# The shared pass up to unit 28 put under manual order with a second table of steps

## The chip, the cores and the metric

The kernel runs on one core of one Trainium2 chip. The metric is the device time of one execution in microseconds (us). The core has five engines with a queue each that runs in order: TensorE (PE; its weight loads are shown as PEld), VectorE (DVE), ScalarE (ACT), GpSimd (POOL) and SyncE (SP), which issues all DMAs here.

## The reference

Four batches of 576 rows with 8 heads of 64 columns go through an attention layer and two feed-forward layers. All is float32, and every large product is made of three matmul passes over high and low halves.

```python
# attention, per batch and head
s = scale * q @ k.T, only where |i - j| < 4        -> softmax -> @ v        # local
q_d, k_d, v_d = means over 4 rows; softmax(q_d @ k_d.T) @ v_d, each row repeated 4 times
x = local + repeated
# layer 1
xn = (x - mean) / sqrt(var + 1e-6) * g_ln
x = x + relu(xn @ w_ch1) @ w_ch2                   # 512 -> 2048 -> 512
# layer 2
h = relu(x.T @ w_tok1) @ w_tok2; u = x + h.T       # 576 -> 256 -> 576
out = u + relu(u @ w_ch1) @ w_ch2                  # 512 -> 1536 -> 512
```

## The kernel before

**Attention** goes by 16 pairs (batch, two heads), n = 0 to 15. Each pair has the steps q_sums and v_sums (GpSimd adds groups of four rows), s_pe (local scores on TensorE), s_max (VectorE), s_exp (ScalarE), d_pe, d_max, d_exp (the same for the means), t_pe and td_pe (transposes), t_copy and td_copy (ScalarE), avd_pe and avd_norm (values of the means), up_write and up_read (a round trip through the DRAM tensor up_scr that repeats the rows), av_pe and av_norm (local values), av_add (GpSimd adds into x).

**Layers 1 and 2** go by 18 chunks of 256 rows, 9 for each layer. A unit is 128 hidden columns of one chunk: g1 (12 matmuls of 128x256, line 629, into a bank of the ring h), a relu on ScalarE (line 635) and its low half on VectorE (line 636), then g2 (6 matmuls of 128x512, line 650, into acc or k). The sequence starts with the shared pass: chunks 0 and 1 in turn with weight unit m = 0 to 13, so that each weight unit is used twice soon after it is made (units 0 to 27), then units 28 to 31 with m = 14 and 15, then chunk by chunk, 252 units in all.

**Weights** arrive as raw 64-bit numbers, 32 pieces of 512 KB for layer 1 (two to a weight unit; piece 2m serves g1, piece 2m + 1 serves g2). A piece is converted in five steps: c_a, c_b, c_c (VectorE, lines 149, 154, 159), c_hi (ScalarE, line 164), c_lo (VectorE, line 167). Raw pieces share three staging buffers, and c_c is the last to read one.

**Order.** A block under `tc.manual_schedule()` gives each engine its instructions in program order. It runs the table START: pairs 0 to 3, pair 4 up to its transposes, the layer norm and transposes of chunks 0 and 1, and pieces 0 to 3. "fill" in it is a matmul without a reader. All else is put in order by the planner of the framework, by program position and by the times that it plans with; it may place such instructions in holes of the manual block. `put(pos, ...)` hangs a step at a unit, and LATER spreads the steps of the pairs over ranges of units. PSUM has four rings of two banks: acc, h, g, k. In the shared pass after START all steps of pairs take banks from g.

```python
for i, (u0, u1) in enumerate(LATER):
    e = later.index((a_values, NP * (i + 2) - 1)) + 1
    for k, (f, n) in enumerate(later[o:e]):
        put(u0 + k * (u1 - u0) / (e - o), f, n)
    o = e
```

Of the kernel before, what the change touches and what calls it, by code (L numbers as in the profile page):

```python
# [8 lines left out]
F32R = mybir.dt.float32r  # L9
I32 = mybir.dt.int32  # L10
ACTF = mybir.ActivationFunctionType
ALU = mybir.AluOpType
# [79 lines left out]
def block_kernel(ctx: ExitStack, tc: tile.TileContext, qk, vw, vg, g_ln, wa, t1, t2, wb, band, out):  # L92
# [215 lines left out]
    def d_pe(n, tag=None):  # L308
        qkd = sts[n].pop("qkd")
        pss = []  # L310
        for h in range(2):
            ps = psg(tag)
            psv = ps[:HG, :2 * SG].rearrange("q (c k) -> q c k", c=2)
            pss.append(psv)
        for c in range(2):
            for h in range(2):
                d = slice(64 * h, 64 * h + 64)
                nc.tensor.matmul(  # L318
                    out=pss[h][:, c, :], lhsT=qkd[d, 0, c * HG:(c + 1) * HG], rhs=qkd[d, 1, :],
                    start=True, stop=True,  # L320
                )
        ld.pop((n, "qk"))
        pending[n, "d"] = pss
# [157 lines left out]
    def av_norm(n, *gs):  # L481
        z = rz[n % 2].unsqueeze(3)
        if gs[0] == 0:
            pending[n, "tmp"] = buf(n, "pt").rearrange("p (t h d) -> p t h d", t=NTL, h=2)
        tmp = pending[n, "tmp"]
        parts = [x for g in gs for x in pending.pop((n, "v", g))]
        for rows, tls, psv in parts:
            nc.vector.tensor_scalar(
                out=z[rows, tls], in0=psv[rows, :, :, D:D + 1], scalar1=1e-9, scalar2=None, op0=ALU.add
            )  # L490
        tls = slice(parts[0][1].start, parts[-1][1].stop)
        nc.vector.reciprocal(out=z[:, tls], in_=z[:, tls])  # L492
        for rows, tls, psv in parts:
            if n < NP:
                shape = [rows.stop - rows.start, tls.stop - tls.start, 2, D]
                nc.vector.tensor_tensor(
                    out=tmp[rows, tls], in0=psv[rows, :, :, :D], in1=z[rows, tls].to_broadcast(shape), op=ALU.mult
                )
                continue
# [122 lines left out]
    def g1(i):  # L622
        c, m = seq[i]
        w = wunit(c, m)
        hp = ps_h.tile([128, 512], F32, tag="h", name="h")
        n = 0
        for kk in range(KD):
            for a, e in PASSES:
                nc.tensor.matmul(  # L629
                    out=hp[:, :CN], lhsT=w[:, 0, a, kk * 128:(kk + 1) * 128], rhs=xT[c][:, kk, e, :],  # L630
                    start=(n == 0), stop=(n == 3 * KD - 1),
                )
                n += 1
        t = ht_p.tile([128, 2, CN], F32R, tag="ht", name="ht")
        nc.scalar.activation(out=t[:, 0], in_=hp[:, :CN], func=ACTF.Relu)  # L635
        nc.vector.scalar_tensor_tensor(  # L636
            out=t[:, 1], in0=hp[:, :CN], scalar=0.0, in1=f32(t[:, 0]), op0=ALU.max, op1=ALU.subtract
        )
        hT[i] = t

    def g2(i):
        c, m = seq[i]
# [130 lines left out]
        base.append(base[-1] + nunits(c))  # L773

    def put(pos, f, *args):
        u, half = divmod(int(2 * pos), 2)
        u = min(u, NSEQ - 1)
        (bg if half else mid)[u].append(lambda: f(*args))

# [51 lines left out]
    def load(n, tag):  # L831
        att_load(n, tag)
# [9 lines left out]
        nc.sync.dma_start(out=grow, in_=g_ln)  # L842
        nc.sync.dma_start(out=mask[:, 1], in_=band[:, 1])

    def s_first(n):
        if n == NP:
            nc.vector.tensor_copy(maskr[1], mask[:, 1])
        s_pe(n, "h")

    def add_run(n, k):  # L850
        if n == NP - 1:
            av_add(n, slice(0, 1) if k == 0 else slice(1, 2), nc.vector)
            if k == 1:
# [9 lines left out]
    def conv_step(k):  # L863
# [7 lines left out]
        q_sums, v_sums, s_max, s_exp, d_max, d_exp, t_pe, t_copy, td_pe, td_copy, avd_pe, avd_norm, up_write,  # L871
        up_read, av_pe, av_norm, load, fill, consts, ln_center, xt_pe, xt_hi, xt_lo,
    )}
    steps.update(
        s_pe=s_first, d_pe=lambda n: d_pe(n, "k"), av_add=add_run, raw=load_unit, st=w_load,
        **{name: conv_step(k) for k, name in enumerate(("c_a", "c_b", "c_c", "c_hi", "c_lo"))},
    )
    with tc.manual_schedule():
# [31 lines left out]
    put(2 * UA - 1.5, rota.__setitem__, slice(None), ["g", "k"])  # L910


    later = []
    for n in range(START_PAIRS, len(order) + 1):
        a = [(f, n) for f in (a_scores, a_down, a_turn, a_turn_down)] if n < len(order) else []
        v = [(f, n - 1) for f in (a_values_down, a_values)] if n > START_PAIRS else []
        later += a[:1] + v[:1] + a[1:2] + v[1:] + a[2:]
    o = 0
    for i, (u0, u1) in enumerate(LATER):
        e = later.index((a_values, NP * (i + 2) - 1)) + 1  # L920
        for k, (f, n) in enumerate(later[o:e]):
            put(u0 + k * (u1 - u0) / (e - o), f, n)
        o = e
# [124 lines left out]
```

## Time and profile before

| what | us |
|---|---|
| median of 3 runs (947.05 to 951.1) | 950.93 |
| the profiled execution, its own time | 952.27 |
| its span, first to last instruction | 950.5 |
| TensorE busy | 916.2 |
| VectorE busy | 447.9 |
| ScalarE busy | 280.6 |
| GpSimd busy | 147.5 |

The span is what the views divide; the execution's own time is 1.77 us longer. Busy time of TensorE counts a matmul at either clock, so a stretch at a low clock is full and slow.

### The profile page before, as it was taken

The numbers are of one execution on the slowest core, as the hardware profiler recorded it, in microseconds if no ns is written. First come the engines' busy times: TensorE is split into PE (matmuls) and PEld (weight loads), VectorE is DVE, ScalarE is ACT, GpSimd is POOL, SyncE is SP. The second block draws the span as 40 slices with busy tenths as digits, with TensorE's granted clock in tenths as the row PEclk, the third lists the DMA queues.
The fourth block names the chain that finished last, engine by engine and source line by source line (L and its number), as shares of the span: only waits on it lengthen the run. The fifth ranks groups of instructions, "written<-read, shape, count | busy, mean of one in ns | idle before, by whom it ended". The sixth has DMA issues, their size and how long they took to land.

```text
span 950.5 us, 17304 instructions
## 1 busy us (share of the span) xinstructions
PE 916.2 (96%) x6702; PEld 801.0 (84%) x6702; DVE 447.9 (47%) x1044; ACT 280.6 (30%) x809; POOL 147.5 (16%) x176
## 2 busy tenths in 40 slices
PE   7879999899999999999999999999999999999998
PEld 5667878778888888888889988787888888999997
DVE  4785788794225252276312267896322322222211
ACT  5444344344443343323111122332112111111111
POOL 6443214213322221111010000111001000000000
PEclk9888999999999999999999999999999999999999
DMA  8653565534232132234212025663212211110100
GB/s 221 183 188 115 157 194 182 169 104 106 83 105 67 47 104 62 67 106 144 73 28 63 23 83 150 190 187 111 57 44 63 51 36 33 45 35 13 44 23 23
DMA packets 113121, 89.78 MB, mean 94 GB/s; under 512 B 73264, under 2 KB 91952, under 8 KB 113040
## 3 DMA queue, kind: packets, MB, share of 16 engines
q1 hardware_dynamic: 113040, 88.68, 32.7%
q8 instruction: 53, 0.87, 0.4%
q14 instruction: 28, 0.23, 0.1%
HBM read 66.62 MB, written 14.16 MB: 85 GB/s over the span
## 4 chain that ended last, share of the span: by engine, by line
PE 78%; DVE 8%; DMA 8%; SPq 2%; ACT 1%; issue 1%; POOL 1%; DVEq 0%; ACTq 0%
PE h L629 33%; PE acc L650 31%; DMA up_scr<-od 2%; DMA st<-in_wb_dram 2%; PE k L650 2%; PE k L729 2%; SPq L586 2%; DMA xr<-x_scr 2%; DVE cv L159 2%; PE g L760 2%; DVE cv L154 1%; PE g L282 1%; PE g L363 1%; PE g L318 1%; PE g L468 1%
## 5 line engine op out<-in xcount | busy, mean ns | idle before, releaser
L629 PEld LDWEIGHTS h<-xt,w 128*128 128x128 f32 x3024 | 395.5, 190 | 25.0 <-ACT w L164 1.9
L629 PE MATMUL h<-xt,w 128*128 128x256 f32 x3024 | 411.8, 284 | 1.6 <-ACT w L164 1.0
L650 PE MATMUL acc<-w,ht 128*128 128x512 f32 x1416 | 378.7, 399 | 8.1 <-ACT ht L635 3.6
L650 PEld LDWEIGHTS acc<-w,ht 128*128 128x128 f32 x1416 | 252.2, 189 | 61.5 <-ACT ht L635 5.7
L636 DVE SCALAR_TENSOR_TENSOR ht<-h,ht 128x256 fp32r<-128x256 f32 x252 | 105.8, 421 | 354.6 <-ACT ht L635 354.3
L635 ACT ACTIVATE ht<-h 128x256 fp32r<-128x256 f32 x252 | 96.4, 383 | 394.0 <-PE h L629 370.4
L714 POOL TENSOR_TENSOR xs<-xr,xs 128x512 fp32r<-128x512 f32 x20 | 26.6, 1330 | 292.4 <-ACT xs L713 292.4
L164 ACT ACTIVATE w<-cv 128x512 fp32r<-128x512 f32 x56 | 35.5, 635 | 70.7 <-DVE cv L159 70.5
L346 POOL TENSOR_TENSOR vg<-vg 72x256 f32<-72x256 f32 x39 | 32.8, 841 | 144.7 <-DMA vg<-in_vg_dram 143.5
L167 DVE TENSOR_TENSOR w<-cv,w 128x512 fp32r<-128x512 f32 x56 | 42.6, 764 | 6.4 <-ACT w L164 6.2
L159 DVE SCALAR_TENSOR_TENSOR cv<-st,cv 128x512 int32<-128x512 int32 (+4 forms) x63 | 42.8, 684 | 0.6
L154 DVE SCALAR_TENSOR_TENSOR cv<-st,cv 128x512 int32<-128x512 int32 (+4 forms) x63 | 42.4, 677 | 0.7
L515 POOL TENSOR_TENSOR x<-x,pt 128x256 f32<-128x256 f32 (+2 forms) x44 | 28.0, 649 | 80.2 <-DMA x<-up_scr 47.9
L729 PE MATMUL k<-xs,t1w 128*128 128x512 f32 (+1 forms) x120 | 33.5, 410 | 2.2 <-ACT xs L713 1.4
L760 PE MATMUL g<-r,t2w 128*128 128x512 f32 x120 | 34.0, 395 | 0.0
L593 ACT ACTIVATE xt<-xt 128x512 fp32r<-128x512 f32 x30 | 19.0, 632 | 50.0 <-DMA xt<-xc 49.9
L149 DVE TENSOR_SCALAR cv<-st 128x512 int32<-128x512 int32 (+4 forms) x63 | 25.8, 412 | 13.8 <-DMA st<-in_wb_dram 8.9
L594 DVE TENSOR_TENSOR xt<-xt 128x512 fp32r<-128x512 f32 x30 | 20.6, 686 | 23.6 <-ACT xt L593 23.5
L650 PE MATMUL k<-w,ht 128*128 128x512 f32 x96 | 27.6, 409 | 0.1
L729 PEld LDWEIGHTS k<-xs,t1w 128*128 128x128 f32 (+1 forms) x120 | 19.1, 188 | 7.2 <-ACT xs L713 2.1
L502 ACT ACTIVATE pt<-g,rz 128x64 f32<-128x64 f32 (+1 forms) x78 | 17.4, 322 | 23.2 <-DVE rz L492 21.8
L760 PEld LDWEIGHTS g<-r,t2w 128*128 128x128 f32 x120 | 20.9, 189 | 3.0
(160 smaller groups left out, 700.6 us busy)
## 6 DMA issues: line engine op xcount, KB each, us to landing
st<-in_wa_dram SPq DMA_DIRECT2D x28, 512.0 KB
st<-in_wb_dram SPq DMA_DIRECT2D x24, 512.0 KB
xt<-xc SPq DMA_DIRECT2D x480, 16.0 KB
qk<-in_qk_dram SPq DMA_DIRECT2D x13, 579.0 KB
x_scr<-x SPq DMA_DIRECT2D x18, 256.0 KB
x<-x_scr SPq DMA_DIRECT2D x9, 512.0 KB
out_dram<-x SPq DMA_DIRECT2D x18, 256.0 KB
vw<-in_vw_dram SPq DMA_DIRECT2D x13, 319.9 KB
```

The costliest lines, as they stand in the source:

```text
L154: nc.vector.scalar_tensor_tensor(out=f, in0=h, scalar=-0x40000000, in1=f, op0=ALU.bitwise_and, op1=ALU.bitwise_or)
L159: nc.vector.scalar_tensor_tensor(out=f, in0=l, scalar=29, in1=f, op0=ALU.logical_shift_right, op1=ALU.bitwise_or)
L164: nc.scalar.activation(out=hi, in_=f.bitcast(F32), func=ACTF.Copy)
L167: nc.vector.tensor_tensor(out=lo, in0=f.bitcast(F32), in1=f32(hi), op=ALU.subtract)
L346: nc.gpsimd.tensor_tensor(out=vd[:, :, :, :D], in0=vd[:, :, :, :D], in1=vgt[:, :, o:o + 128].rearrange("p c (h d) -> p c h d", h=2), op=AL ...
L515: (eng or nc.gpsimd).tensor_tensor(out=x, in0=x, in1=tmp[rows, tl:tl + k].rearrange("p t h d -> p t (h d)"), op=ALU.add)
L629: nc.tensor.matmul(out=hp[:, :CN], lhsT=w[:, 0, a, kk * 128:(kk + 1) * 128], rhs=xT[c][:, kk, e, :], start=(n == 0), stop=(n == 3 * KD - 1),)
L635: nc.scalar.activation(out=t[:, 0], in_=hp[:, :CN], func=ACTF.Relu)
L636: nc.vector.scalar_tensor_tensor(out=t[:, 1], in0=hp[:, :CN], scalar=0.0, in1=f32(t[:, 0]), op0=ALU.max, op1=ALU.subtract)
L650: nc.tensor.matmul(out=acc[c, j], lhsT=t[:, a, j * 128:(j + 1) * 128], rhs=w[:, 1, e, :], start=(m == 0 and n == 0), stop=(last and n == 2),)
L729: nc.tensor.matmul(out=rps[b, m], lhsT=tokw["t1"][rows, a, n, m * 128:(m + 1) * 128], rhs=t[rows, e, :], start=(n == 0 and i == 0), stop=( ...
L760: nc.tensor.matmul(out=ps, lhsT=tokw["t2"][:, a, m, o:o + 128], rhs=r_t[b][:, m, e, :], start=(i == 0), stop=(i == len(ops) - 1),)
```

## The change

START stays. A second table, PASS, follows it in the same manual block. It holds pair 4 from avd_pe on, the pairs 5, 6 and 7 whole, pieces 4 to 31 (their raw loads from piece 7 on and their conversions), the loads of pair 8, g1, relu and low of units 0 to 28, and g2 of units 0 to 27. So relu and low become steps of their own, and so does av_act, the part of av_norm that runs on ScalarE for pairs from 4 on. d_pe of pairs 5 to 7 takes its banks from g, as s_pe does. The loop over units starts at 28, and whatever was hung at an earlier unit (the layer norm and the first transposes of chunk 2) is hung at 28. ln_rstd of chunks 0 and 1 was hung at units 8 and 10 and now stands right behind the block. The steps of the pairs from 8 on are spread over units 28 to 51 and 52 to 82; a_scores and a_down of pair 8 were in the range 1 to 25.

```diff
-LATER = ((1, 25), (26, 51), (52, 82))
+PASS = """
+    g1 0; g1 1; avd_pe 4; relu 0; c_a 4; relu 1; c_b 4; q_sums 5; low 0; low 1; g2 0; c_c 4; avd_norm 4;
+    c_hi 4; raw 3 1; g1 2; c_a 5; up_write 4; c_lo 4; v_sums 5; g2 1; relu 2; c_b 5; low 2; c_c 5; av_pe 4;
+    c_a 6; c_hi 5; raw 4 0; c_b 6; g1 3; c_lo 5; av_z 4; up_read 4; g2 2; relu 3; c_c 6; av_act 4; low 3;
+    c_a 7; g1 4; raw 4 1; c_b 7; c_c 7; c_hi 6; s_pe 5 g; relu 4; raw 5 0; c_lo 6; c_hi 7; g2 3; low 4;
+    av_add 4; s_max 5; g1 5; c_lo 7; s_exp 5; c_a 8; g2 4; c_b 8; c_c 8; relu 5; d_pe 5 g; c_a 9; c_hi 8;
+    raw 5 1; low 5; g1 6; load 6 qk; c_b 9; d_max 5; g2 5; relu 6; low 6; d_exp 5; c_lo 8; g1 7; c_c 9; c_a
...
+    25; relu 26; low 26; c_hi 30; c_a 31; g1 27; c_lo 30; c_b 31; g2 26; relu 27; c_c 31; low 27; c_hi 31;
+    g1 28; c_lo 31; g2 27; relu 28; low 28
+"""
+PASS_UNITS = 28
+
+LATER = ((28, 51), (52, 82))
...
+    def relu(i):
+        hT[i] = t = ht_p.tile([128, 2, CN], F32R, tag="ht", name="ht")
+        nc.scalar.activation(out=t[:, 0], in_=hps[i][:, :CN], func=ACTF.Relu)
+
+    def low(i):
+        hp, t = hps.pop(i), hT[i]
...
     def put(pos, f, *args):
-        u, half = divmod(int(2 * pos), 2)
+        u, half = divmod(int(2 * max(pos, PASS_UNITS)), 2)
...
+        emit(START)
         load(5, "vg")
         load(5, "vw")
+        rota[:] = ["g"]
+        emit(PASS)
     for c in range(2):
-        put(8 + 2 * c, ln_rstd, c)
-    rota[:] = ["g"]
-    a_values_down(NP)
-    a_values(NP)
-    for u in range(2 * UA):
-        bg[u].append(lambda: w_split(NPC // 2))
+        ln_rstd(c)
+    nl[0] = nsp[0] = len(pieces)
...
-    for n in range(START_PAIRS, len(order) + 1):
+    for n in range(2 * NP, len(order) + 1):
...
-    g1(0)
-    for i in range(NSEQ):
+    for i in range(PASS_UNITS, NSEQ):
         if i + 1 < NSEQ:
-            g1(i + 1)
+            for f in (g1, relu, low):
+                f(i + 1)
```

## Rows read from the trace of the kernel before

**Rows 1.** The page: busy time and share of TensorE.

```profile
PE 916.2 (96%) x6702; PEld 801.0 (84%) x6702; DVE 447.9 (47%) x1044; ACT 280.6 (30%) x809; POOL 147.5 (16%) x176
```

**Rows 2.** Windows by stage: busy time of each engine, granted clock, DMA.

```profile
240.00:400.00 160.00, 160.00 (x1407) 140.92 (x1405) 55.97 (x162) 59.46 (x205) 33.12 (x49) 1.00 0.28 75
```

**Rows 3.** Windows in the shared pass: PE, PEld, DVE, ACT, POOL busy, clock.

```profile
86.70:93.80 7.10, 7.10 (x21) 5.36 (x22) 6.16 (x12) 3.85 (x12) 4.67 (x2) 0.53 0.43 143
93.80:188.50 94.70, 88.00 (x740) 75.00 (x739) 76.88 (x167) 40.92 (x120) 29.20 (x28) 1.00 0.56 176
sum 119.00, PE 110.18 PEld 93.56 DVE 91.23 ACT 50.96 POOL 35.94; mean PE 27.54 PEld 23.39 DVE 22.81 ACT 12.74 POOL 8.99
```

**Rows 4.** Waits of TensorE, 69.5 to 188.5 us: total, times, longest.

```profile
PE g L318 <- issue: 2.1, 1, 2.1
...
PE acc L650 <- ACT w L164: 1.7, 3, 0.9
```

**Rows 5.** Timeline of TensorE: start, us, what, idle before.

```profile
86.68 2.23 PE L318 MATMUL g<-qkd 64*72 64x144 f32 x8 [2.12 <-issue]
...
186.47 0.73 PE L650 MATMUL acc<-w,ht 128*128 128x512 f32 x2 [1.76 <-ACT ht L635]
```

**Rows 6.** Window around the gap before 186.47 us.

```profile
185.00:187.00 2.00, 0.53 (x2) 0.30 (x2) 1.97 (x4) 1.06 (x3) 0.00 (x0) 1.00 0.25 53
```

**Rows 7.** Timeline of ScalarE: s_exp of pair 5.

```profile
85.42 2.20 ACT L300 ACTIVATE sm<-g,nm 128x70 f32<-128x70 f32 x10 [2.42 <-DVE nm L292]
```

**Rows 8.** Timeline of TensorE: one whole unit without gaps.

```profile
136.56 1.60 PE L629 MATMUL h<-xt,w 128*128 128x256 f32 x12
138.00 1.55 PE L650 MATMUL k<-w,ht 128*128 128x512 f32 x6
139.38 0.63 PE L629 MATMUL h<-xt,w 128*128 128x256 f32 x4
```

**Rows 9.** Windows of line 629 alone (g1): TensorE busy and count.

```profile
0.00:69.50 69.50, 6.06 (x36) 4.91 (x36) 0.90 0.72 202
```

**Rows 10.** Timeline of TensorE at the end of START.

```profile
64.75 0.59 PE L837 MATMUL acc<-mask,ident 128*128 128x256 f32 x2
65.00 1.89 PE L629 MATMUL h<-xt,w 128*128 128x256 f32 x13
67.70 0.26 PE L384 MATMUL g<-ident,attw 72*72 72x72 f32 x1 [0.82 <-ACT attw L337]
67.89 1.45 PE L629 MATMUL h<-xt,w 128*128 128x256 f32 x10
...
69.36 0.41 PE L384 MATMUL acc<-ident,attw 72*72 72x72 f32 x4
```

**Rows 11.** Timelines of VectorE and ScalarE there: low 0, d_max 4, d_exp 4.

```profile
63.36 0.41 DVE L636 SCALAR_TENSOR_TENSOR ht<-h,ht 128x256 fp32r<-128x256 f32 x1
...
65.94 0.81 DVE L328 TENSOR_REDUCE dm<-k 72x2 f32<-72x288 f32 x2
...
67.27 1.18 ACT L337 ACTIVATE attw<-k,dm 72x144 f32<-72x144 f32 x4 [1.64 <-DVE dm L329]
```

**Rows 12.** Groups by line, VectorE, 69.5 to 188.5: c_a of staged pieces.

```profile
L149 DVE TENSOR_SCALAR cv<-st 128x512 int32<-128x512 int32 x26 | 11.0, 425 | 3.1 <-DMA st<-in_wa_dram 3.1
```

**Rows 13.** Timeline of VectorE: first two steps of ln_rstd.

```profile
107.69 0.16 DVE L556 TENSOR_SCALAR va<-mv 128x2 f32<-128x2 f32 x1
107.88 0.17 DVE L558 TENSOR_SCALAR y<-va 128x2 int32<-128x2 int32 x1
```

**Rows 14.** Timeline of TensorE: chunk 2's second transposes and first g1.

```profile
208.11 0.66 PE L573 MATMUL g<-ident,xc 128*128 128x128 f32 x4 [0.28 <-ACT sm L300]
...
210.78 0.48 PE L629 MATMUL h<-xt,w 128*128 128x256 f32 x2
```

**Rows 15.** By line over the whole run: duration in ns, min/median/max.

```profile
L262 POOL TENSOR_TENSOR qkd<-qkd,qk x13: 932/947/3857, 5.6 to 349.5; 128x288 f32<-128x288 f32 x13
...
L154 DVE SCALAR_TENSOR_TENSOR cv<-st,cv x63: 218/682/1802, 70.0 to 650.4; 128x512 int32<-128x512 int32 x52, 128x256 int32<-128x256 int32 x5, 128x288 int32<-128x288 int32 x2, 128x224 int32<-128x224 int32 x2
```

More of the change, by code (lines that the diff above doesn't have):

```diff
@@ L66 @@
 """
-LATER = ((1, 25), (26, 51), (52, 82))
+PASS = """
[5 more added lines that the diff above has]
+    raw 5 1; low 5; g1 6; load 6 qk; c_b 9; d_max 5; g2 5; relu 6; low 6; d_exp 5; c_lo 8; g1 7; c_c 9; c_a
+    10; c_hi 9; raw 6 0; t_pe 5 0; c_b 10; t_pe 5 1; relu 7; t_copy 5 0; c_lo 9; g2 6; t_copy 5 1; low 7;
+    c_c 10; q_sums 6; t_pe 5 2; td_pe 5 0; t_copy 5 2; c_a 11; g1 8; raw 6 1; td_copy 5 0; c_b 11; c_hi 10;
+    c_c 11; td_pe 5 1; relu 8; c_lo 10; g2 7; raw 7 0; td_copy 5 1; c_hi 11; low 8; c_a 12; avd_pe 5; c_lo
+    11; c_b 12; g1 9; load 6 vg; avd_norm 5; c_c 12; av_pe 5; up_write 5; relu 9; c_a 13; c_hi 12; low 9;
+    raw 7 1; c_b 13; g2 8; load 6 vw; av_z 5; v_sums 6; c_lo 12; g1 10; av_act 5; c_c 13; g2 9; c_a 14;
+    up_read 5; c_b 14; relu 10; c_c 14; c_hi 13; s_pe 6 g; low 10; raw 8 0; c_hi 14; c_lo 13; g1 11; raw 8
+    1; s_max 6; g2 10; relu 11; c_lo 14; s_exp 6; low 11; av_add 5; g1 12; c_a 15; c_b 15; c_c 15; d_pe 6 g;
+    relu 12; c_a 16; c_hi 15; raw 9 0; g2 11; low 12; load 7 qk; d_max 6; g1 13; c_lo 15; d_exp 6; c_b 16;
+    g2 12; relu 13; c_c 16; low 13; c_hi 16; raw 9 1; t_pe 6 0; c_a 17; c_b 17; t_pe 6 1; t_copy 6 0; g1 14;
+    c_lo 16; t_copy 6 1; c_c 17; q_sums 7; t_pe 6 2; relu 14; td_pe 6 0; c_a 18; raw 10 0; t_copy 6 2; g2
+    13; low 14; td_copy 6 0; c_b 18; c_hi 17; c_c 18; td_pe 6 1; g1 15; td_copy 6 1; c_lo 17; raw 10 1; c_hi
+    18; c_a 19; c_lo 18; avd_pe 6; relu 15; low 15; g2 14; c_b 19; load 7 vg; avd_norm 6; g1 16; c_c 19;
+    up_write 6; c_a 20; c_hi 19; c_b 20; av_pe 6; raw 11 0; relu 16; c_lo 19; v_sums 7; low 16; g2 15; load
+    7 vw; c_c 20; av_z 6; c_hi 20; raw 11 1; g1 17; c_a 21; up_read 6; av_act 6; c_lo 20; g2 16; c_b 21; c_c
+    21; relu 17; s_pe 7 g; c_a 22; c_hi 21; raw 12 0; low 17; c_b 22; g1 18; s_max 7; g2 17; relu 18; c_lo
+    21; s_exp 7; low 18; av_add 6; g1 19; c_c 22; c_a 23; raw 12 1; c_b 23; c_hi 22; d_pe 7 g; relu 19; c_c
+    23; g2 18; load 8 qk; low 19; c_hi 23; raw 13 0; d_max 7; g1 20; c_lo 22; d_exp 7; c_lo 23; g2 19; relu
+    20; c_a 24; low 20; t_pe 7 0; c_b 24; t_pe 7 1; t_copy 7 0; c_c 24; g1 21; t_copy 7 1; c_a 25; raw 13 1;
+    c_hi 24; c_b 25; t_pe 7 2; relu 21; c_lo 24; td_pe 7 0; t_copy 7 2; g2 20; td_copy 7 0; low 21; c_c 25;
+    td_pe 7 1; c_a 26; c_hi 25; raw 14 0; g1 22; c_b 26; td_copy 7 1; c_lo 25; avd_pe 7; relu 22; c_c 26;
+    low 22; g2 21; c_hi 26; raw 14 1; c_a 27; load 8 vg; avd_norm 7; g1 23; c_lo 26; up_write 7; c_b 27;
+    av_pe 7; relu 23; c_c 27; low 23; c_hi 27; raw 15 0; c_a 28; g2 22; load 8 vw; c_b 28; av_z 7; g1 24;
+    c_lo 27; av_act 7; c_c 28; up_read 7; g2 23; c_a 29; c_b 29; relu 24; c_c 29; g1 25; raw 15 1; c_hi 28;
+    low 24; c_hi 29; c_lo 28; g2 24; relu 25; c_lo 29; low 25; g1 26; c_a 30; av_add 7; c_b 30; c_c 30; g2
+    25; relu 26; low 26; c_hi 30; c_a 31; g1 27; c_lo 30; c_b 31; g2 26; relu 27; c_c 31; low 27; c_hi 31;
+    g1 28; c_lo 31; g2 27; relu 28; low 28
@@ L492, in av_norm, with av_act @@
         nc.vector.reciprocal(out=z[:, tls], in_=z[:, tls])
+        if n >= NP:
+            pending[n, "z"] = parts
+            return
         for rows, tls, psv in parts:
[L494 to L499, printed above, removed]
+            shape = [rows.stop - rows.start, tls.stop - tls.start, 2, D]
+            nc.vector.tensor_tensor(
+                out=tmp[rows, tls], in0=psv[rows, :, :, :D], in1=z[rows, tls].to_broadcast(shape), op=ALU.mult
+            )
+    def av_act(n):
+        z = rz[n % 2].unsqueeze(3)
+        tmp = pending[n, "tmp"]
+        for rows, tls, psv in pending.pop((n, "z")):
             for tl in range(tls.start, tls.stop):
@@ L524, in a_values @@
         av_norm(n, 0, 1)
+        av_act(n)
         av_add(n)
@@ L616, in block_kernel @@
     hT = {}
+    hps = {}
     acc = {}
@@ L633, in g1 @@
                 n += 1
-        t = ht_p.tile([128, 2, CN], F32R, tag="ht", name="ht")
-        nc.scalar.activation(out=t[:, 0], in_=hp[:, :CN], func=ACTF.Relu)
+        hps[i] = hp
+    def relu(i):
[3 more added lines that the diff above has]
+        hp, t = hps.pop(i), hT[i]
         nc.vector.scalar_tensor_tensor(
@@ L638, in g1 @@
         )
-        hT[i] = t
     def g2(i):
@@ L843, in consts, with s_first, add_run @@
         nc.sync.dma_start(out=mask[:, 1], in_=band[:, 1])
-    def s_first(n):
+    def s_first(n, tag="h"):
         if n == NP:
             nc.vector.tensor_copy(maskr[1], mask[:, 1])
-        s_pe(n, "h")
-    def add_run(n, k):
-        if n == NP - 1:
+        s_pe(n, tag)
+    def add_run(n, k=None):
+        if k is None:
+            av_add(n)
+        elif n == NP - 1:
             av_add(n, slice(0, 1) if k == 0 else slice(1, 2), nc.vector)
@@ L873, in block_kernel, with av_pes, emit @@
     )}
+    def av_pes(n, g=None):
+        for k in range(2) if g is None else (g,):
+            av_pe(n, k)
     steps.update(
-        s_pe=s_first, d_pe=lambda n: d_pe(n, "k"), av_add=add_run, raw=load_unit, st=w_load,
+        av_pe=av_pes, s_pe=s_first, d_pe=lambda n, tag="k": d_pe(n, tag), av_add=add_run, raw=load_unit, st=w_load,
         **{name: conv_step(k) for k, name in enumerate(("c_a", "c_b", "c_c", "c_hi", "c_lo"))},
     )
+    steps.update(
+        g1=g1, relu=relu, low=low, g2=g2, av_z=lambda n: av_norm(n, 0, 1), av_act=av_act,
+    )
+    def emit(table):
+        for step in table.split(";"):
+            name, *args = step.split()
+            steps[name](*(int(a) if a.isdigit() else a for a in args))
     with tc.manual_schedule():
@@ L897, in block_kernel @@
         nl[0] = nsp[0] = EARLY * NPC
-        for step in START.split(";"):
-            name, *args = step.split()
-            steps[name](*(int(a) if a.isdigit() else a for a in args))
+        emit(START)
         load(5, "vg")
         load(5, "vw")
+        rota[:] = ["g"]
+        emit(PASS)
     for c in range(2):
-        put(8 + 2 * c, ln_rstd, c)
-    rota[:] = ["g"]
-    a_values_down(NP)
-    a_values(NP)
-    for u in range(2 * UA):
-        bg[u].append(lambda: w_split(NPC // 2))
+        ln_rstd(c)
+    nl[0] = nsp[0] = len(pieces)
     put(2 * UA - 1.5, rota.__setitem__, slice(None), ["g", "k"])
     later = []
-    for n in range(START_PAIRS, len(order) + 1):
+    for n in range(2 * NP, len(order) + 1):
         a = [(f, n) for f in (a_scores, a_down, a_turn, a_turn_down)] if n < len(order) else []
-        v = [(f, n - 1) for f in (a_values_down, a_values)] if n > START_PAIRS else []
+        v = [(f, n - 1) for f in (a_values_down, a_values)] if n > 2 * NP else []
         later += a[:1] + v[:1] + a[1:2] + v[1:] + a[2:]
@@ L919, in block_kernel @@
     for i, (u0, u1) in enumerate(LATER):
-        e = later.index((a_values, NP * (i + 2) - 1)) + 1
+        e = later.index((a_values, NP * (i + 3) - 1)) + 1
         for k, (f, n) in enumerate(later[o:e]):
```

## The prediction

> **What bounds the kernel now.** I read four views in this order. The page's busy shares come first: TensorE is busy 916.2 of 950.5 us [rows 1], so at most 34 us can be won by filling its gaps, wherever they lie. The windows by stage come second: from 240 to 400 us TensorE is busy 160.00 of 160 us [rows 2], so nothing that only moves work into that stretch can help, and every us that the shared pass saves earlier comes off the end, as long as TensorE stays full behind it. The shared pass up to unit 28 lies almost wholly between 69.5 and 188.5 us. There TensorE is busy 110.18 of 119 us, and VectorE 91.23, GpSimd 35.94 [rows 3]: TensorE is the bound, VectorE (which must make 28 half weight units for it) is second. Third, the waits of TensorE in that stretch say what ends its 8.8 us of gaps: one of 2.1 us before the downsampled scores (L318), one of 1.76 us behind a relu [rows 5], most of the rest before weights that were still being converted [rows 4]. Fourth, the granted clock. In 86.7 to 93.8 us it is 0.53, that is mostly at the 1.2 GHz level, right behind the gap of 2.1 us; in the rest of the pass it is 1.00 [rows 3]. Those 7.1 us did 7.1 x 0.53 = 3.8 us of work at 2.4 GHz, so the low clock cost 3.3 us. The gap of 1.76 us at 184.7 to 186.5 left the clock at 1.00 [rows 5, 6].
>
> **What the change does, part by part.** It adds no arithmetic: units, conversions, pairs and loads are the same instructions. It fixes their order on each queue. So the price is in gaps and clock.
>
> The gap before d_pe 5 goes. Scores s_pe 5 and d_pe 5 both use the two banks named g, so d_pe must wait for s_exp 5 on ScalarE, which runs 2.20 us from 85.42 to 87.62 [rows 7]; s_pe 5 had ended where the gap begins, 2.12 before 86.68 [rows 5], so 3.1 us earlier. In the table g2 3, g1 5 and g2 4 stand between s_pe 5 and d_pe 5. A g1 takes 1.44 us (start 136.56 to 138.00) and a g2 1.38 (138.00 to 139.38) [rows 8], in sum 4.2 us, over the 3.1 needed. The same pattern stands before d_pe 6 and 7. Won: 2.1 of gap and 3.3 of clock, 5.4 us. If s_max 5 came 1.1 us late on VectorE, the cover would be gone and each us more would be a gap.
>
> The other gaps, 8.8 - 2.1 = 6.7 us, are mostly a conversion that came just in time or late. The table starts piece 4 at once and has c_lo of a piece one and a half to four units ahead of the g1 or g2 that reads it, 4 to 11 us at 2.82 a unit. Bounds: all 6.7 won, or none, if real waits break the order as often as before. The engines have room (VectorE 91 of the 107 us that TensorE needs without gaps and low clock), but a fixed queue waits where a planned time was short, and nothing passes the waiting instruction: behind a low that waits for its relu stand the next conversions, and the raw load that c_c would free. I take a third, 2.2 us, as still lost.
>
> The start of the pass gets worse. The first table is under manual order too, and up to now the planner put units that were not under it into its holes: 36 matmuls of g1 (three units) ran before 69.5 us [rows 9], 13 of them behind the last fill at 64.75 and 10 between the first and the last transposes td_pe 4 [rows 10]. Now g1 0 stands in the same fixed order behind td_pe 4 1. Those transposes wait for d_exp 4 on ScalarE (67.27 to 68.45), which waits for d_max 4 on VectorE at 65.94 [rows 11]. The low 0 that stood in front of it at 63.36, 0.34 us to the next start, moves behind, so td_pe 4 can be done at about 68.5 instead of 69.6. The 36 matmuls at 0.12 us are 4.3 us of work that now come later; 1.1 us of it is given back. Lost: 3.2 us.
>
> And TensorE now stands idle there. The fills end between 64.0 (no g1 in front of them) and 65.2 (as now), the first transpose can run at about 67.3. That is a hole of 2.1 to 3.3 us, where the rows show a low clock behind 2.1 and none behind 1.76 [rows 3, 5, 6]. So the cost is 0 or about the 3.3 us of the stretch at 86.7; I take 3.3, since nearly all of the estimated hole lies above the gap that did it.
>
> The SyncE queue: raw loads, writes and reads of the upsampled rows and pair loads stay on one queue, in an order that was the planner's and is now the table's. A read of up_scr waits for the write to land, and the raw load behind it waits too; VectorE once waited 3.1 us for such a load [rows 12], which stands behind the late weights of the 1.76 us gap [rows 5]. In the table one or two raw loads stand between up_write and up_read, so this is part of the 2.2 above and has no term of its own.
>
> Work is moved behind the pass: ln_rstd of chunks 0 and 1 (24 small steps on VectorE whose starts lie about 0.2 us apart [rows 13], so some 4.8 us if they run one after the other), ln_center, the transposes and split of chunk 2, and a_scores and a_down of pair 8, which used to run inside the pass. Chunk 2 starts after three more units. Until then TensorE has g1 29 to 31 and g2 28 to 31, 3 x 1.44 + 4 x 1.38 = 9.8 us [rows 8], and pair 8's scores; the split of chunk 2 must queue on VectorE behind ln_rstd and share the bank ring g with pair 8. In the run before, the second transpose of chunk 2 waited on that ring for s_exp, and the chunk's first g1 came only 2.7 us later, hidden by other pair work [rows 14]. Bounds: 0 (hidden again), or about 6 (a gap of 2.7 and a low clock of 3.3 behind it). Nearest is the row with the cover; I take 1.0. Pair 8's matmuls are only moved, at no price, since TensorE is full in 240 to 400 [rows 2]. av_z and av_act, relu and low are the old lines under new names and cost nothing.
>
> One price could be larger than the rows' means. GpSimd's second add of q_sums takes 0.93 to 3.86 us, and a conversion step (L154) up to 1.80 at a median of 0.68 [rows 15]: the two engines hold each other up. The Trainium skill says so as a rule (SBUF — State Buffer, section "Who interferes with whom"): a VectorE instruction with two SBUF inputs and a GpSimd instruction that reads SBUF take turns, and the second waits for the whole of the first. By it alone the two would exclude each other, which is the second rival below; the trace agrees in the outliers, while the medians show that most instructions don't meet.
>
> **The sum.** Won 2.1 + 3.3 + 6.7 = 12.1. Lost 3.2 + 3.3 + 2.2 + 1.0 = 9.7. Net 2.4 us off the profiled execution's own 952.27, 949.9. The median of the runs before lies 1.34 below that execution, so 948.5 against 950.93.
>
> **The rivals.**
>
> *The order holds and the clock stays up.* If the hole at the start stays under what lowers the clock, 3.3 comes back, and with fewer waits in the pass up to 2.2 more and the 1.0 at its end: 942 to 945, say 943.5. For it: piece times in the table have 4 to 11 us of lead, and the first transposes can start on d_exp's first parts. Against: the 2.1 us gap in the rows was enough.
>
> *VectorE becomes the bound (slower).* If GpSimd's work stopped VectorE for its whole length, the pass would need 91.2 + 35.9 = 127 us of VectorE. The forecast pass, on the old window's work, takes 119 - 12.1 + 3.2 + 3.3 + 2.2 = 115.6. So from 24 of GpSimd's 36 us on, VectorE decides, and in full it costs 11.5 more: 960; at two thirds to all of it, 949 to 960, with the gaps' own low clock (3.3 each) on top; say 957. For it: the table fixes which conversion stands beside q_sums and v_sums, and in-order queues hand each delay on. Against: VectorE's 91.2 holds the blocked time of this run already.
>
> *The gain is handed back at chunk 2, or the change does not shorten the pass.* A gap plus low clock at the hand-over (6 instead of 1.0), or 6.7 us of new waits for the old ones (2.2 more than half), takes the 2.4 away: 951 to 953.
>
> **How the numbers follow.** Forecast 0.36 (its own range 946 to 951), clock stays up 0.27, VectorE bound 0.22, handed back 0.15. A difference under 0.5% (4.75 us) is about what a measurement of this kernel can't tell from no change. Faster: all of the second case and 0.08 of the forecast's low end, 0.35. Slower: all of the VectorE case and 0.03 of the last, 0.25. Same: 0.40. The range must reach into the cases of both signs: 940 (12.1 - 3.2 + the clock kept, nearly nothing else lost) to 957, leaving about 0.08 below and 0.12 above.
>
> **What would show it.** Right: TensorE's first h matmul of the pass at 68 to 69 us with none before it, a hole of 2 to 3 us ahead of it and a clock of about 0.5 for some 7 us; no gap before d_pe 5, 6, 7; at most 2 to 3 us of gaps from 75 us to g2 27; TensorE full again up to 400. Wrong: h matmuls ahead of td_pe 4 (then the start costs nothing), VectorE over 95% busy in the pass, gaps of over 2 us with a low clock behind them in the pass or before unit 32, or a different stretch behind 400 us.

## The result, and the profile after

The changed kernel takes 938.35 us (median of 4 runs, 933.4 to 939.4), the kernel before 950.44 (4 runs, 947.05 to 951.1): a ratio of 0.987, 95% interval 0.9827 to 0.9912. It is 1.3% faster. The forecast was 948.5 with a range of 940 to 957, so the time lies just below the range. The profiled execution took 939.0 with a span of 936.9, and 13.6 us of span have to be explained (950.5 to 936.9) where the forecast had 2.4.

The page of the changed kernel, busy time and share of each engine (before: [rows 1]):

```profile
PE 909.1 (97%) x6702; PEld 797.1 (85%) x6702; DVE 448.0 (48%) x1044; ACT 281.3 (30%) x809; POOL 141.5 (15%) x176
```

TensorE is busy 7.1 us less, at the same 6702 matmuls. So only about half of the 13.6 us is idle time that was filled; the rest is time in which TensorE was busy before and is not any more. Windows by stage (busy time of PE, PEld, DVE, ACT, POOL, then granted clock, DMA share, GB/s) say where. First the kernel before, then the changed one:

```profile
75.00:180.00 105.00, 98.20 (x788) 83.19 (x785) 82.29 (x183) 47.15 (x145) 32.27 (x30) 0.97 0.52 160
180.00:200.00 20.00, 16.87 (x137) 13.97 (x136) 16.74 (x32) 8.72 (x27) 6.60 (x9) 1.00 0.38 126
```

```profile
75.00:180.00 105.00, 104.24 (x928) 91.12 (x927) 96.70 (x203) 52.58 (x160) 28.69 (x34) 1.00 0.59 184
180.00:200.00 20.00, 17.63 (x128) 14.62 (x127) 13.01 (x31) 6.69 (x19) 2.69 (x3) 0.83 0.21 64
```

In the same 105 us of the shared pass TensorE now gets through 928 matmul records instead of 788. The pass has almost no gaps and a clock of 1.00. Behind it, from 180 to 200, lies the stretch that got worse most: 2.4 us idle and a clock of 0.83.

The pass itself, from its first unit to g2 27, holds the same unit matmuls in both kernels (348 of g1, of which 36 lay before 69.5 us in the kernel before [rows 9], and 168 of g2). Windows of just that stretch, before and after:

```profile
69.50:191.20 121.70, 112.88 (x931) 95.97 (x928) 93.86 (x207) 52.27 (x161) 36.42 (x34) 0.97 0.52 162
```

```profile
66.13:174.40 108.27, 107.51 (x948) 94.67 (x945) 97.13 (x196) 53.15 (x157) 28.81 (x35) 0.98 0.58 178
```

Idle time fell from 8.8 to 0.8 us. And the busy time fell too. Before: 112.9, plus 4.3 for the 36 early matmuls, less 3.3 for the low clock [rows 3], less 2.1 for what has no counterpart in the window after (8 downsampled-score matmuls of pair 8, ten of its score matmuls, which now run at 176 us, and td_pe 4), makes 111.8. After: 107.5 less 1.7 for a low clock at its start makes 105.8. So the same matmuls take 6.0 us less. The 1.7 us are half of the 3.4 us from 66.8 to 70.2 that ran at 0.50; the ends follow from the granted clocks 0.91 and 0.88 of these windows (TensorE alone: busy, granted clock, DMA):

```profile
66.00:67.00 1.00, 1.00 (x12) 0.91 0.08 16
...
70.00:71.00 1.00, 1.00 (x12) 0.88 0.00 0
```

Which ones shows the timeline of TensorE (start, us, what and how many, idle before). The kernel before, around the scores of pair 6 and one half of its downsampled scores:

```profile
100.89 0.32 PE L273 MATMUL g<-maskr,identr 128*128 128x350 f32 x1
101.14 0.83 PE L282 MATMUL g<-qk 64*64 64x70 f32 x18
101.90 0.62 PE L629 MATMUL h<-xt,w 128*128 128x256 f32 x3
102.36 0.33 PE L273 MATMUL g<-maskr,identr 128*128 128x350 f32 x1
102.61 0.83 PE L282 MATMUL g<-qk 64*64 64x70 f32 x18
...
110.15 0.71 PE L318 MATMUL g<-qkd 64*72 64x144 f32 x4
```

The changed kernel, pair 5:

```profile
81.64 0.48 PE L309 MATMUL g<-maskr,identr 128*128 128x350 f32 x2
82.05 0.84 PE L318 MATMUL g<-qk 64*64 64x70 f32 x36
82.82 1.66 PE L699 MATMUL k<-w,ht 128*128 128x512 f32 x6
84.31 1.60 PE L673 MATMUL h<-xt,w 128*128 128x256 f32 x12
85.75 1.55 PE L699 MATMUL acc<-w,ht 128*128 128x512 f32 x6
87.23 0.71 PE L354 MATMUL g<-qkd 64*72 64x144 f32 x8
```

In pairs 5 to 7, thirty-six score matmuls now take what eighteen took, and eight of the downsampled scores what four took. The planner had done the 18 of one head, then other work, then the 18 of the other; the table runs them as the program writes them, head 0 and head 1 in turn. A head has 64 of the array's 128 rows, and the two heads lie in different halves. So two matmuls of different heads run at the same time, if they stand next to each other. The Trainium skill (TensorE: Matmul & The Clock Gate, section "Part 3: Packing small matmuls — row/col tiling") says that matmuls on different row groups of the array overlap; this trace agrees: 0.77 us from start to next start for 36, against 0.76 for 18.

The same lines over 0 to 420 us, the scores and then the downsampled scores (sums of a windows view of one line each), before:

```profile
sum 420.00, PE 20.04 PEld 16.48; mean PE 6.68 PEld 5.49
...
sum 420.00, PE 18.14 PEld 11.54; mean PE 6.04 PEld 3.85
```

and after:

```profile
sum 420.00, PE 17.48 PEld 14.03; mean PE 5.83 PEld 4.68
...
sum 420.00, PE 14.50 PEld 8.82; mean PE 4.83 PEld 2.94
```

That is 6.2 us less, of which about 1 is the low clock that d_pe 5 ran at before [rows 5]. Some of it lies behind the pass, in pairs 9 and 10, where the planner happened to keep the heads together. Pair 8 gained nothing: its scores are not in the table, and the planner spread them in seven groups from 161 to 176.5 us.

### The profile page after: what moved, and what is told of

The parts are those of the page before. It is cut to its first block, busy times and chain, and to the rows that moved or that the text cites. A ratio compares the mean times of both kernels' runs of the same rounds, so it can differ in the third digit from the quotient of the medians.

```text
span 936.9 us, 17322 instructions
## 1 busy us (share of the span) xinstructions
PE 909.1 (97%) x6702; PEld 797.1 (85%) x6702; DVE 448.0 (48%) x1044; ACT 281.3 (30%) x809; POOL 141.5 (15%) x176
## 4 chain that ended last, share of the span: by engine, by line
PE 74%; DVE 11%; DMA 7%; SPq 3%; issue 1%; POOL 1%; ACT 1%; DVEq 0%; ACTq 0%; POOLq 0%
PE h L673 32%; PE acc L699 30%; DVE cv L195 2%; DMA st<-in_wb_dram 2%; SPq L629 2%; DVE cv L190 2%; PE k L778 2%; DMA up_scr<-od 2%; PE g L809 2%; DVE cv L185 1%; DMA xr<-x_scr 1%; PE k L699 1%; DMA x<-up_scr 1%; DVE ht L686 1%; DVE w L203 1%
## 5 line engine op out<-in xcount | busy, mean ns | idle before, releaser
L195 DVE SCALAR_TENSOR_TENSOR cv<-st,cv 128x512 int32<-128x512 int32 (+4 forms) x63 | 45.7, 728 | 0.8
L382 POOL TENSOR_TENSOR vg<-vg 72x256 f32<-72x256 f32 x39 | 28.8, 737 | 105.1 <-DMA vg<-in_vg_dram 103.5
L203 DVE TENSOR_TENSOR w<-cv,w 128x512 fp32r<-128x512 f32 x56 | 40.4, 723 | 5.6 <-ACT w L200 5.5
L190 DVE SCALAR_TENSOR_TENSOR cv<-st,cv 128x512 int32<-128x512 int32 (+4 forms) x63 | 42.4, 675 | 0.9
L185 DVE TENSOR_SCALAR cv<-st 128x512 int32<-128x512 int32 (+4 forms) x63 | 30.2, 481 | 11.9 <-DMA st<-in_wb_dram 9.2
L637 DVE TENSOR_TENSOR xt<-xt 128x512 fp32r<-128x512 f32 x30 | 20.5, 685 | 24.1 <-ACT xt L636 23.4
```

The costliest lines, as they stand in the source:

```text
L185: return nc.vector.tensor_scalar(out=f, in0=h, scalar1=3, scalar2=0x3FFFFFFF, op0=ALU.logical_shift_left, op1=ALU.bitwise_and)
L190: nc.vector.scalar_tensor_tensor(out=f, in0=h, scalar=-0x40000000, in1=f, op0=ALU.bitwise_and, op1=ALU.bitwise_or)
L195: nc.vector.scalar_tensor_tensor(out=f, in0=l, scalar=29, in1=f, op0=ALU.logical_shift_right, op1=ALU.bitwise_or)
L203: nc.vector.tensor_tensor(out=lo, in0=f.bitcast(F32), in1=f32(hi), op=ALU.subtract)
L382: nc.gpsimd.tensor_tensor(out=vd[:, :, :, :D], in0=vd[:, :, :, :D], in1=vgt[:, :, o:o + 128].rearrange("p c (h d) -> p c h d", h=2), op=AL ...
```

## The experiments

Two theories stood against each other. Theory A: TensorE's time is its matmuls' own time plus its waits; the table removed the waits and put the two heads side by side, lost a few us at each end of the pass, and each of these items counts for itself, so that each can be taken away or won back alone. Theory B, the rival: only waits count (or VectorE, nearly always busy, sets the pace); what is shortened at one place comes back as a wait at the next, and shorter score matmuls are a side effect. Each run's ratio is to the kernel before on the same chip. Where two runs come from different chips, the difference of their ratios stands for the difference in time, and by the intervals such a difference is good to some 3 to 3.5 us.

### The changed kernel again

> The changed kernel once more, to be run beside the three edits of it. In its first profile the first h matmul of the pass stood at 66.1 us, 2.4 earlier than forecast, and the kernel before had its last transposes td_pe 4 at 69.4. Theory A, START is shorter because the planner no longer places other work into it: the pass begins again at 66 to 67. Theory B, START ends where the round trips through up_scr happen to land: it begins anywhere from 65 to 70. Time 938 by both, plus or minus 3.

Measured: 940.48 us (937.15 to 943.58) against 951.52, 0.9879 (0.9852 to 0.9905). The gain is repeated. The pass begins at 69.26 us this time, so theory B holds: the 66.13 of the first profile belongs to that execution. The hole before td_pe 4 is there again at the same length (timeline of TensorE):

```profile
67.89 1.14 PE L420 MATMUL g<-ident,attw 72*72 72x72 f32 x4 [3.02 <-ACT attw L373]
```

### The heads apart

```diff
-        for i in range(NB):            # s_pe, pairs 5 to 7
-            for h in range(2): ...
+        for h in range(2):
+            mask matmul of head h
+            for i in range(NB): ...
-        for c in range(2):             # d_pe
-            for h in range(2): ...
+        for h in range(2):
+            for c in range(2): ...
```

> One thing undone: s_pe and d_pe of pairs 5 to 7 issue all matmuls of one head and then all of the other, as the kernel before did, instead of head by head in turn. Theory A, the turn of heads (64 rows each, the two halves of the array) lets the two run side by side and saved about 0.9 us in s_pe and 0.6 in d_pe per pair: 4 to 5 us slower than the changed kernel, about 943; s_pe 2.0 to 2.1 instead of 1.2 us, d_pe 1.3 instead of 0.65. Theory B, the whole gain came from gaps and low clock, and the order of heads is of no account: within 1 us of the changed kernel.

Measured: 942.60 us (939.52 to 945.0), 0.9894 (0.9867 to 0.9921), 2.1 us over the changed kernel on the same chip, between the two theories. The two sets of runs overlap, so the time alone is weak; the timeline is not:

```profile
84.34 0.32 PE L310 MATMUL g<-maskr,identr 128*128 128x350 f32 x1
84.59 0.83 PE L326 MATMUL g<-qk 64*64 64x70 f32 x18
85.35 0.43 PE L310 MATMUL g<-maskr,identr 128*128 128x350 f32 x1
85.71 0.83 PE L326 MATMUL g<-qk 64*64 64x70 f32 x18
86.47 1.66 PE L708 MATMUL k<-w,ht 128*128 128x512 f32 x6
...
90.86 0.72 PE L363 MATMUL g<-qkd 64*72 64x144 f32 x8
```

The scores take 2.13 us from 84.34 to 86.47 instead of 1.18 (81.64 to 82.82). The mask matmul between the heads uses all 128 rows; that it is what keeps the second head from starting is my reading, since no run has the heads one after the other with both masks ahead of them. The downsampled scores did not get longer: two groups of four, head after head but with nothing between, still take 0.66 us (90.86 to 91.52). So for s_pe the order of the heads, with the mask that it puts between them, is the cause; d_pe had cost 1.3 before with the two groups set apart in time by the planner.

### The scores in turns, in the order of before

```diff
 def s_pe(n, tag=None):          # the kernel before, no second table
+    if n >= START_PAIRS:
+        with tc.manual_schedule():
+            s_mm(n, tag)        # the old body; d_pe the same
```

> The kernel before, with nothing of the table; only s_pe and d_pe of pairs from 5 on stand each in a manual block of their own, so that the heads go in turn. Theory A, shorter score matmuls are a part of the gain that needs no table: 0.85 us for s_pe of 6 pairs and some 0.5 for d_pe of 5, so 5 to 7 us under the kernel before. Theory B, waiting for two free banks makes new gaps for what the matmuls save: within 2 us of the kernel before.

Measured: 955.45 us (12 runs, 953.26 to 959.89) against 952.50, 1.0045 (1.0025 to 1.0065): 3 us slower, which lies in neither theory's range, and far from theory A's. The matmuls did get shorter: from start to next start, without idle time and low clock, the scores of pairs 5 to 10 took 5.1 us less and the downsampled ones 1.2. Shorter matmuls alone bought nothing here. The longest entries of TensorE's waits from 60 to 215 us (total, times, longest), and its pass:

```profile
PE acc L664 <- ACT ht L649: 4.7, 3, 3.2
PE acc L664 <- ACT w L164: 3.4, 2, 3.0
PE g L332 <- ACT sm L307: 3.1, 2, 2.5
```

```profile
75.00:180.00 105.00, 94.08 (x780) 79.78 (x779) 81.94 (x178) 45.89 (x142) 31.21 (x29) 0.95 0.51 158
```

What the scores saved came back as idle time before weights, a relu and the banks of s_exp (L332 is d_pe): 10.9 us of it in this window against 6.8 in the kernel before, and a clock of 0.95 against 0.97. That the heads pay only where the order has something ready to put in their place fits this, but it was not tested alone: the manual blocks also changed what the planner could place around them.

### The end of START

```diff
-fill; d_max 4; fill; c_lo 2; d_exp 4; fill; c_c 3; td_pe 4 0; ...
+fill; d_max 4; fill; c_lo 2; d_exp 4; fill; g1 0; g1 1; c_c 3; td_pe 4 0; ...
-g1 0; g1 1; avd_pe 4; relu 0; ...
+avd_pe 4; relu 0; ...
```

The changed kernel has the hole that the forecast named. Timeline of TensorE there:

```profile
61.29 0.70 PE L886 MATMUL acc<-mask,ident 128*128 128x256 f32 x2
65.02 1.06 PE L420 MATMUL g<-ident,attw 72*72 72x72 f32 x4 [3.02 <-ACT attw L373]
65.92 0.41 PE L420 MATMUL acc<-ident,attw 72*72 72x72 f32 x4
66.13 4.61 PE L673 MATMUL h<-xt,w 128*128 128x256 f32 x24
```

> g1 0 and g1 1 moved from the head of PASS to before td_pe 4 in START, into the hole of 3.0 us in which TensorE waits for d_exp 4. Theory A, TensorE's order sets the time of the pass: the hole and the low clock behind it (3.9 us at 1.2 GHz, 2.0 us lost) go, 3 to 5 us faster than the changed kernel, about 934. Theory B, VectorE (97 to 98% busy from 90 to 160 us in the changed kernel) sets it: the units start sooner and then wait for weights, new gaps of TensorE from 90 us on, within 1.5 us of the changed kernel.

Measured: 937.94 us (935.28 to 939.81), 0.9847 (0.9822 to 0.9873), 2.5 us under the changed kernel on the same chip, between the two theories, and the two sets of runs overlap. The hole is filled by g1 0 and g1 1, but a low clock stayed:

```profile
63.86 3.22 PE L673 MATMUL h<-xt,w 128*128 128x256 f32 x24
67.28 1.06 PE L420 MATMUL g<-ident,attw 72*72 72x72 f32 x4 [0.20 <-ACT attw L373]
69.06 1.38 PE L443 MATMUL g<-attw 72*72 72x65 f32 x16 [0.47 <-issue]
```

Windows of 1 us there show 0.70 from 70 to 71, 0.50 from 71 to 73 and 0.59 from 73 to 74, so the low clock lasts from about 70.4 to 73.8. By these runs, mending the hole is worth some 2 to 3 us, not 5.

### The hand-over to chunk 2

```diff
-    g1 28; c_lo 31; g2 27; relu 28; low 28
+    g1 28; c_lo 31; g2 27; relu 28; low 28; ln_center 2 0; g1 29; ln_center 2 1;
+    xt_pe 2 0; relu 29; xt_hi 2 0; g2 28; low 29; xt_lo 2 0; xt_pe 2 1; xt_hi 2 1; xt_lo 2 1
-PASS_UNITS = 28                                  # and bufs=2 for mv
+PASS_UNITS = 29                                  # and bufs=4
...                                               # chunk 2's steps are no longer hung at units
```

In the changed kernel the second transposes of chunk 2 wait for the banks that d_exp 8 reads, and a little later pair 8's transposes for VectorE (timeline of TensorE):

```profile
186.45 0.71 PE L354 MATMUL g<-qkd 64*72 64x144 f32 x4
...
188.99 0.66 PE L616 MATMUL g<-ident,xc 128*128 128x128 f32 x4 [1.84 <-ACT pd L373]
...
191.00 0.69 PE L420 MATMUL k<-ident,pd 72*72 72x72 f32 x4 [0.53 <-DVE x L707]
```

and the clock falls (windows of 1 us, TensorE alone: busy, granted clock):

```profile
189.00:190.00 1.00, 1.00 (x7) 0.85 0.13 20
190.00:191.00 1.00, 0.47 (x3) 0.50 0.00 0
...
196.00:197.00 1.00, 1.00 (x8) 0.73 0.11 17
```

> ln_center, transposes and split of chunk 2, g1 29 and g2 28 appended to the table (with two more small buffers for the statistics), so that the second transpose of chunk 2 does not wait for a bank of g behind d_exp of pair 8. Theory A, the gaps of 1.8 and 0.5 us and the low clock from 189.8 to 196.5 us stand behind that bank: they go, 4 to 6 us faster than the changed kernel, about 933. Theory B, VectorE with ln_rstd of two chunks is late in any order, and the gap only moves: within 1.5 us of the changed kernel.

Measured: 933.89 us (932.93 to 935.53), 0.9808 (0.9785 to 0.9831), 6.6 us under the changed kernel on the same chip, with no run of one set inside the other. The stretch is full:

```profile
180.00:200.00 20.00, 20.00 (x174) 17.47 (x173) 15.61 (x48) 7.27 (x25) 2.76 (x3) 1.00 0.36 101
```

The hand-over cost 1.84 + 0.53 idle and 3.2 for the low clock from 189.7 to 196.5 us, 5.5 us; the rest of the 6.6 is within the runs' spread.

### Both ends mended

```diff
-fill; d_max 4; fill; c_lo 2; d_exp 4; fill; c_c 3; td_pe 4 0; c_hi 3; td_pe 4 1; td_copy 4 0; c_lo 3; ...
+fill; d_max 4; fill; g1 0; c_lo 2; relu 0; d_exp 4; g1 1; fill; low 0; c_c 3; td_pe 4 0; c_hi 3;
+td_pe 4 1; td_copy 4 0; g2 0; c_lo 3; ...        # taken out of PASS; and the edit of the hand-over
```

> The hand-over mended as in e3, and at the start g1 0, relu 0, g1 1, low 0 and g2 0 placed around d_exp 4 and td_pe 4, so that the holes of 0.2 and 0.5 us that e2 still had behind the moved units (and the low clock at 70.7 to 73.8 us behind those) are filled too. Theory A, both ends of the pass are on TensorE's path and add up: 6.6 us of e3 and 2.5 to 4 of the start, 929 to 932 against 940.5 for the changed kernel. Theory B, what the start wins is waited for later on VectorE: no better than e3, 933 to 935.

Measured: 930.26 us (928.4 to 930.65) against 952.50, 0.9766 (0.9739 to 0.9792). The ratio is 0.0113 under that of the changed kernel (0.9879, on another chip), 10.7 us; the hand-over alone gave 6.6, and the start 2.5 in its first form. Within the spread the two add up, as theory A has it.

### The later pairs in turns too

```diff
 def s_pe(n, tag=None):          # on top of both ends mended
+    if n >= 2 * NP:
+        with tc.manual_schedule():
+            s_mm(n, tag)        # d_pe the same
```

> e5, and s_pe and d_pe of the pairs from 8 on each in a manual block of their own, so that the planner can not set the heads apart. Theory A, the turn of heads is worth 0.85 us in s_pe of pairs 8 to 10 and 0.6 in d_pe of those that stand apart: 3 to 5 us under e5. Theory B, s_pe must now wait until two banks are free and the planner loses its fillers: within 1 us of e5, or slower.

Measured: 926.83 us (924.17 to 928.68), 0.9732 (0.9704 to 0.9760), 3.4 us under the last one on the same chip; only one of its six runs reaches into the other's five. Behind the pass TensorE is full (219.4 of 220 us from 180 to 400), and the shorter matmuls pay: from start to next start, the scores of pairs 8 to 10 took 2.3 us less. The downsampled ones took no less, since the planner still put other matmuls between their two groups; the other 1.1 us are not assigned. This version beats both kernels: by 2.7% the one before, and, by the two ratios (0.9732 / 0.9879, on different chips), by 1.5% the changed one.

### VectorE loaded

```diff
         conv[p][k]()
+        if k == 1 and p >= EARLY * NPC:
+            conv[p][k]()        # c_b a second time, same operands, same result
```

> The changed kernel with step c_b of pieces 4 to 31 done twice (the second changes nothing in the data): 28 more VectorE instructions of 0.65 us, 18 us in all. Theory A, TensorE sets the pass and VectorE has some room left, about 8 us of the 105 between 75 and 180 us: 6 to 11 us slower than the changed kernel, with new waits of TensorE for weights. Theory B, VectorE at 97 to 98% already sets the pass: the whole 16 to 18 us slower. Theory C, the lead of the conversions hides it all: under 3 us.

Measured: 952.38 us (12 runs, 948.76 to 958.45) against 952.50, 0.9999 (0.9979 to 1.0019). That is 0.0120 over the changed kernel's ratio (from another chip), 11.4 us: at the upper end of theory A, clear of theory B. What was added shows in VectorE's groups by line from 60 to 200 us (count | busy, mean ns | idle before), here and in the changed kernel:

```profile
L190 DVE SCALAR_TENSOR_TENSOR cv<-st,cv 128x512 int32<-128x512 int32 x56 | 41.8, 747 | 1.5
```

```profile
L190 DVE SCALAR_TENSOR_TENSOR cv<-st,cv 128x512 int32<-128x512 int32 x28 | 21.3, 762 | 0.5
```

The 28 more took 20.5 us and cost 11.4, so about 9 us of them cost no time. TensorE's pass now, and its longest waits:

```profile
75.00:180.00 105.00, 94.67 (x839) 82.00 (x839) 99.79 (x191) 48.20 (x145) 30.08 (x34) 0.96 0.59 183
```

```profile
PE acc L699 <- DVE ht L686: 3.1, 1, 3.1
PE g L504 <- DVE od L456: 2.9, 2, 1.9
PE g L309 <- DVE cv L190: 1.5, 1, 1.5
```

Now it is VectorE that TensorE waits for, in lines that hardly wait in the changed kernel, where TensorE idles 0.76 us in this stretch.

### No cover between the scores

```diff
-... c_hi 7; g2 3; low 4; av_add 4; s_max 5; g1 5; c_lo 7; s_exp 5; c_a 8; g2 4; c_b 8; c_c 8; relu 5; d_pe 5 g; ...
+... c_hi 7; low 4; av_add 4; s_max 5; c_lo 7; s_exp 5; c_a 8; c_b 8; c_c 8; d_pe 5 g; g2 3; g1 5; g2 4; relu 5; ...
```

> The changed kernel with the cover of one wait taken away: g2 3, g1 5 and g2 4 stand behind d_pe 5 instead of before it, so d_pe 5 must wait for s_exp 5 as in the kernel before; the order on the other engines is the same. Theory A, a hole of 2 to 3.5 us and the low clock behind it (3.3 us) come back whole: 4.5 to 6.5 us slower than the changed kernel. Theory B, VectorE (only some 6 us of room by the run with the doubled step) gains the lead that TensorE loses, so TensorE makes up part of it: 1 to 3 us slower.

Measured: 945.39 us (942.14 to 945.96) against 950.68, 0.9927 (0.9903 to 0.9951): 0.0048 over the changed kernel's ratio (from another chip), 4.6 us. That favours theory A, but the spread of such a difference reaches into theory B. Timeline of TensorE:

```profile
82.44 0.84 PE L318 MATMUL g<-qk 64*64 64x70 f32 x36
86.38 0.59 PE L354 MATMUL g<-qkd 64*72 64x144 f32 x2 [3.09 <-ACT sm L336]
87.38 1.23 PE L354 MATMUL g<-qkd 64*72 64x144 f32 x6 [0.41 <-ACT sm L336]
```

Holes of 3.09 and 0.41 us and a clock of 0.50 up to 93: the wait of [rows 5] is back, at the length that the forecast gave it (3.1).

### The kernel before, once more

> The kernel before once more, for a second look at where START ends. Theory A, work that the planner placed into START makes it longer: td_pe 4 starts at 67 to 68 again, against 63.2 to 67.9 in the profiles with the table. Theory B, the spread of the round trips through up_scr is the same in both: anywhere from 63 to 68.

Measured, one run: 954.68 us, span 952.9. The last transposes td_pe 4 start at 69.63 us, later than either theory said; where START ends spreads by more than both. The gap of 2.12 before d_pe 5 is there again, at 88.60 us (86.68 in [rows 5]), so it belongs to the order and is no accident of one execution. The gap of 1.76 [rows 5] is 2.95 us here, and this time a low clock follows it (0.50 from 188 to 194).

## Why the prediction was wrong

The sign of the sum was right, and most terms were. By its own steps:

- **"The gap before d_pe 5 goes", 5.4 us: right.** TensorE goes from s_pe 5 through g2 3, g1 5 and g2 4 into d_pe 5 without a gap (82.82 to 87.23, 4.4 us of cover). Without the cover 4.6 us came back, give or take some 3.4.
- **"I take a third, 2.2 us, as still lost": too much.** 0.76 us of idle are left from 75 to 180 us, 1.4 better.
- **The start: mechanism right.** No g1 stands before td_pe 4, the hole is 3.02 us (2.1 to 3.3 forecast), and a low clock follows. In the first profile it lasted 3.4 us instead of some 7 and cost 1.7 instead of 3.3; of the six profiles with this hole (2.71 to 3.03 us) three show 3.4 us of it and three 6.8, so the size was right in half of them. The first g1 came at 66.13 us, not at 68 to 69, and in the other five at 64.53 to 69.26. How far this is the table's doing stays open: td_pe 4 starts at 67.23, 67.70 and 69.63 in three profiles with the order of before and at 63.17 to 67.89 in six with that of the changed kernel's START; about 2.5 us earlier on average, but they overlap.
- **Chunk 2, "I take 1.0": the mechanism was right and the size off.** The wait on the bank ring and the low clock behind it cost 5.5 us, close to the upper bound of "about 6". The row that I called nearest [rows 14] had other pair work as cover; as I read it, the table had moved that work away.
- **The step that failed: "It adds no arithmetic [...] So the price is in gaps and clock."** It took TensorE's 107 us of matmuls as fixed. The same matmuls took 6.0 us less in the pass, and about 4.1 less behind it, where the forecast has nothing but the hand-over. I count each from its start to the next one's start, without idle time and low clock (the sums of a view by line count overlaps twice). In the pass, pairs 5 to 7 saved 2.7 in the scores with their masks and 1.8 in the downsampled scores, and pair 8 lost 0.6: together some 3.8 of the 6.0. Of the rest, 0.9 lies in the pairs' other small matmuls and 1.3 in g1 of the units. Behind the pass, pairs 9 and 10 saved 2.2 and pair 13 lost 0.3; the other 2.3 lie in many lines. The cause of what isn't scores, 4.5 us in all, stays open: no run tested it.

From the forecast's -2.4 to the span's -13.6: other gaps -1.4, low clock at the start -1.6, the start of the pass earlier in this profile -2.7, TensorE's own time in the pass -6.0, hand-over +4.5, TensorE's own time behind the pass -4.1, other idle time behind it -1.6 (1.0 of it at 400 to 460 us, 58.98 to 60.00 busy of 60), and +1.7 for a low clock at 633 to 637 us, behind a hole of 1.44 and 0.72 us that the kernel before has too, without the low clock. With the -2.4 the sum is -13.6; these are readings of two executions, good to some tenths each, so the exact fit is chance. It is luck, too, that the forecast's range was missed by only 1.7 us: two misses of 10 and 4.5 us went opposite ways.

Of the rivals, "the order holds and the clock stays up" got the pass right, though the clock did fall at both ends, and the gain was larger than its 942 to 945 too. "VectorE becomes the bound" had its sign (98% busy in single stretches, as the window below shows) and not its effect: TensorE waited 0.4 us for it from 75 to 180 us, and about 9 us of added work cost no time. "Handed back at chunk 2" had the size of its loss nearly (5.5 of 6), but the gain above it was several times the 2.4 forecast.

```profile
120.00:130.00 10.00, 10.00 (x101) 8.93 (x101) 9.83 (x20) 3.24 (x8) 2.97 (x4) 1.00 0.60 173
```

## What to carry to other kernels

Equal instruction counts do not make equal TensorE time: where matmuls use half the rows, look in the timeline whether the two halves stand next to each other with no full-height matmul between, and whether a planner has set them apart. Shortening them paid here where the engine was full; where it waited for late inputs, the saving came back as longer waits, so order the inputs first. When an order is fixed by hand for one stretch, look at its two ends: the work that used to cover a wait there may have moved inside, and a hole of 2 us there can cost a low clock too.

## What the runs showed of the hardware

- **The length of a hole did not tell what the clock does.** 1.84 us at 187 to 189 was followed by about 6.8 us at the low level (189.7 to 196.5). Holes of 2.71 to 3.03 us at the end of the same START were followed by 3.4 us of it in three profiles and by 6.8 in three. 1.76 us in the kernel before was followed by none [rows 5, 6]. 1.44 and 0.72 us near 632 were followed by 3.4 in the changed kernel, and the same hole in the kernel before by none. With the start filled, holes of 0.20 and 0.47 us around the small transposes were still followed by 3.4 us (70.4 to 73.8). What sets these cases apart wasn't separated.
- **Two heads in turn took the time of one.** 36 score matmuls of 64 rows took 0.77 us and 18 of one head 0.76; with a full-height mask matmul between the heads the overlap was gone (1.18 to 2.13 us for a pair's scores with their masks).
- **An engine can be 92% to 98% busy and not be the bound.** VectorE at 96.70 of 105 us was given 20.5 us more work, and the kernel took only 11.4 us longer.
